# Planning the filler matmuls of a two-problem sliding-window attention by availability and deadline

## The chip, the cores and the metric

The kernel runs on one core of a Trainium2 chip. Its time is the device time in microseconds (us) of one launch; of several executions the median is given. A profile is one more execution, with the hardware profiler. Engines are named as in the profile: PE is TensorE's matmuls, PEld its weight loads, DVE is VectorE, ACT is ScalarE, POOL is GpSimd, and SP is SyncE, which here only issues DMAs.

## The reference

Two independent attention blocks, A and B, each with its own x (2048 x 1024), wqkv (1024 x 3072) and wo (1024 x 1024) in bf16; their outputs are put side by side into 2048 x 2048:

```
qkv = (x @ wqkv) -> q, k, v      # 32 heads of 32
scores = q k^T / sqrt(32)        # key j is seen by query i for 0 <= i - j < 256, else -1e9
out = softmax(scores) v -> (2048 x 1024) @ wo
```

With blocks of 128 positions, a query block sees its own key block (triangular mask), the one before (whole) and the one before that (the other triangle).

## The kernel before, in words

**Groups and sessions.** A group g is four heads of one problem (128 columns of q and of k), so there are 8 groups a problem and G = 16 in all. Of the 16 x 16 pairs of a key block j and a query block q, 45 are within the window (`entries`, L61). They are taken four at a time: a session. NS = 12 sessions make a group, the last of which has one pair alone, and the whole work is 192 sessions. `session` (L260) multiplies k by q for its four pairs and four heads into the PSUM tile st (one buffer, four banks; at most 32 small matmuls that run four at once in the array's row quarters), has ACT take the exp of all of it into pt (L280), and POOL zero the masked triangles (L285, L289). With one st the next session's scores wait for this exp.

**PV.** Two sessions (PV_LAG) after the last session that a chunk of 512 queries needs (k = 0 to 3, `ready`, L64), `pv` (L293) multiplies pt by V and by ones into the PSUM tile acc (one buffer, two banks), which gives the unnormalized output and the sums. DVE then normalizes in four pieces of 128 columns, a reciprocal (L321) and a multiply (L322) each. The first piece is issued at once; the others wait in the list `side` and are issued one at a time between fillers, after every 700 ns of them, or all together ahead of the next PV. There are 4 PVs in a group, in its sessions 4, 7, 10 and in session 1 of the next.

**Fillers.** All other matmuls (128 x 128 weights, 512 columns, planned at NS_MM = 216 ns) come in chains of 8 that accumulate into one of two PSUM tiles pp: QK chains (L133; 8 a group, one for q and one for k in each chunk of 512 positions, evicted by DVE with a cast, L146, and an OR into `top`, L148, from which `certify` reads at the end whether the values were small enough for an exp without a maximum), V chains (L153; 16 for each superblock m of four groups, evicted by ACT, L167) and output chains (L171; 32 a problem, evicted by ACT, L185, and stored by SP, L187).

**The planner.** TensorE runs in the order that the Python loop writes out. Each chain has a session from which it may start (`early`) and one by which it must be done (`late`); the list is sorted by `late`, and `start_chain` (L225) takes the first that may start. For each session the loop issues in this order: the chains that are due (`forced`), the scores, the PV that is due, the DMAs listed for it (`loads`), and then fillers until their planned time reaches a budget (`emit`, L234). The budget is max(NS_BASE = 1750 ns, `need`), where `need` (L251) is the largest rate that the deadlines ask for; it doesn't count what the session itself holds of scores and PV, nor whether the fillers will last. QK of group g may start with group g - 1, V of superblock m with the group before it, and A's output chains stand before V and QK chains of B by their deadlines. B's output chains have no deadline and begin once the last group's PVs are done; what is left of them when the 192 sessions are over is issued then.

**Loads.** x tiles (512 positions, transposed by the DMA, 1 MB, six buffers) and weights are issued on SP in the order of the listing, but each as soon as its buffer is free and what stands before it in SP's queue is issued. wqk is loaded for two groups at a time (512 KB for q and for k, pieces of 512 bytes); only the first such load is cut in two. At the start, the first half of wqk and V's first weights (1 MB) are issued on ACT's queue while SP issues the x tiles.

Of the kernel before, what the change touches and what calls it, by code (L numbers as in the profile page):

```python
# [18 lines left out]
P = 128  # L19
# [10 lines left out]
NS_BASE = 1750.0  # L30
PV_LAG = 2

# [19 lines left out]
def _fast_path(ctx, tc, cfg, problems, outs, consts, certify):  # L52
# [32 lines left out]
    zt = once.tile([P, 512], BF16, name="zt")  # L85
    nc.vector.memset(zt[:], 0.0)
    top = once.tile([P, 2, 512], BF16, name="top")
    nc.vector.memset(top[:], 0.0)
# [13 lines left out]
    def load_wqk(pair, queue, halves=(0, 1)):  # L102
        pi, t = divmod(2 * pair, T)
        if pair not in wqk:
            wqk[pair] = wqkp.tile([P, CT, 2, 256], BF16, name="wqk")
        if len(halves) == 2:
            cols = [(0, 256)]
        else:
            cols = [(128 * h, 128 * h + 128) for h in halves]
        for lo, hi in cols:  # L110
            for k in range(2):
                queue.dma_start(out=wqk[pair][:, :, k, lo:hi],
                                in_=wsrc(pi)[:, :, k, t * P + lo:t * P + hi])
# [19 lines left out]
    def qk_steps(g, which, k, lo=0, hi=512, st_=None, last=True):  # L133
        pi = g // T
        st_ = {} if st_ is None else st_
        steps = []
        for ct in range(CT):
            def f(ct=ct):
                if "pp" not in st_:
                    st_["pp"] = ps_proj.tile([P, 512], F32, name="pp")  # L140
                w_ = wqk[g // 2][:, ct, which, (g % 2) * P:(g % 2) * P + P]
                nc.tensor.matmul(st_["pp"][:, lo:hi], lhsT=w_, rhs=xT[(pi, k)][:, ct, lo:hi],  # L142
                                 start=(ct == 0), stop=(ct == CT - 1))
                if ct == CT - 1 and last:
                    dst = qk_tiles(g)[which][:, k * 512:(k + 1) * 512]
                    nc.vector.tensor_copy(out=dst, in_=st_["pp"][:])  # L146
                    seen = top[:, which, :].bitcast(I32)
                    nc.vector.tensor_tensor(out=seen, in0=seen, in1=dst.bitcast(I32),  # L148
                                            op=ALU.bitwise_or)
            steps.append((NS_MM * (hi - lo) / 512.0, f))  # L150
        return steps
# [53 lines left out]
    for m in range(NPROB * T // SB):  # L205
        for b in range(NB):
            k = b // QB
            g = m * SB
            early = NS * (g - 1) if k < 2 else pv_time(g - 1, k - 1) + 1
            chains.append(_Chain(early, pv_time(g, k), v_steps(m, b)))  # L210
    for pi in range(NPROB):
        for b in range(NB):
            k = b // QB
            osb = [None]
            early = pv_time(pi * T + T - 1, k) + 2
            late = 10 ** 6
# [4 lines left out]
    chains.sort(key=lambda c: c.late)  # L221

# [11 lines left out]
    def emit(now, budget):  # L234
        done = 0.0
        since = 0.0
        while done < budget and (current or start_chain(now)):
            ns, f = current.pop(0)
            f()
            done += ns  # L240
            since += ns
            if side and since >= 700.0:
                side.pop(0)()
                since = 0.0
        return done

    def forced(now):
        while any(c.late <= now for c in chains) or (current and current[0] is None):
            emit(now, NS_MM * CT if not current else NS_MM * len(current))

    def need(now):  # L251
        rate, work = 0.0, sum(ns for ns, _ in current)
        for c in chains:
            if c.late >= 10 ** 6:
                break
            work += NS_MM * CT
            rate = max(rate, work / (c.late - now)) if c.late > now else rate
        return rate
# [34 lines left out]
    def pv(g, k):  # L293
# [23 lines left out]
        rinv = misc.tile([P, 512], F32, name="rinv")  # L317
        for a in range(QB):
            def f(a=a):
                sl = slice(a * P, (a + 1) * P)  # L320
# [20 lines left out]
    for pair in range(2, G // 2):  # L341
        at(NS * (2 * pair - 2) + 1, lambda pair=pair: load_wqk(pair, nc.sync))
    for m in range(1, NPROB * T // SB):
        at(pv_time(SB * (m - 1), NQ - 1) + 1, lambda m=m: load_wv(m, nc.sync))
    for pi in range(1, NPROB):
        for k in range(NQ):
            now = NS * (pi * T - 3) + 2 * k if k < 2 else NS * (pi * T - 1) + first_use(k - 2, 0) + 1
            at(now, lambda pi=pi, k=k: load_x(pi, k))

    warm = ps_proj.tile([P, 512], F32, name="pp")  # L350
    for _ in range(11):
        nc.tensor.matmul(warm[:], lhsT=zt[:, 0:P], rhs=zt[:], start=True, stop=True)
# [6 lines left out]
    due = [(pv_time(g, k), g, k) for g in range(G) for k in range(NQ)]  # L359
    wo_next = 1  # L360
    certified = False
    for now in range(NS * G):
# [10 lines left out]
        emit(now, max(NS_BASE, need(now)))  # L373
        if not certified and g == G - 1 and not any(c.late < 10 ** 6 for c in chains):
            certify(top, ps_proj)
            certified = True
        if wo_next < NPROB and now >= NS * wo_next * T and not any(
                c.late < pv_time(wo_next * T + 1, 0) + 1 and c.early == pv_time(wo_next * T - 1, NQ - 1) + 2
                for c in chains) and not current:
            load_wo(wo_next)  # L380
            wo_next += 1
    end = NS * G
# [141 lines left out]
def kernel(  # L524
# [29 lines left out]
    def certify(top, pool):  # L554
        seen = top[:].rearrange("p a b -> p (a b)")
        nc.vector.tensor_single_scalar(out=seen.bitcast(I32), in_=seen.bitcast(I32),
                                       scalar=0x7FFF7FFF, op=ALU.bitwise_and)
# [51 lines left out]
```

## Time and profile before

| | |
|---|---|
| median of 3 runs | 739.2 us (737.25 to 740.1) |
| profiled execution | 739.39 us, of which the span from the first to the last instruction is 737.6 |
| PE busy | 646.8 us, 88% of the span |
| DVE, ACT, POOL busy | 449.9, 410.0, 301.5 us |
| mean granted clock of TensorE | 0.948 of full speed |
| time to the first exp, and from the last exp to the end | 19.7 us, 53.2 us |

The profile's page sums each engine's busy time, cuts the span into 40 slices and follows the chain of work that ended last. Queries to the same trace give the busy time in chosen windows, the instructions in order of time, and for each instruction how long its engine had been idle before it and what it waited for (in brackets). A busy PE isn't one at full rate: at half the granted clock the same matmuls are busy twice as long.

### The profile page before, as it was taken

The page shows a single profiled execution, that of the slowest core. Times are in us where ns is not written, and L with a number is a line of the kernel's source. Part 1 is how long each engine was busy: PE and PEld are TensorE (multiplying, and loading weights), DVE is VectorE, ACT ScalarE, POOL GpSimd, SP SyncE. Part 2 cuts the span into 40 slices and gives each one's busy share as a digit, 9 for nine tenths or more (in the row PEclk, how much of TensorE's full clock was granted, in tenths as well). Part 3 has the DMA queues.
Part 4 walks back from the last instruction along what each step waited for, and adds up shares of the span by engine and source line. Part 5 has one row for each costly group of instructions (what it writes and reads, how often), then busy time and mean ns, then how long its engine had stood idle before and what let it go on. Part 6 is the DMA issues. An engine that isn't in the chain of part 4 may idle for free.

```text
span 737.6 us, 15737 instructions
## 1 busy us (share of the span) xinstructions
PE 646.8 (88%) x6877; PEld 295.7 (40%) x6877; DVE 449.9 (61%) x776; ACT 410.0 (56%) x321; POOL 301.5 (41%) x484
## 2 busy tenths in 40 slices
PE   5999999589997867689999998997999998748996
PEld 2444344344443333334444443443444444324442
DVE  1363888665677759456325337997767799865500
ACT  0655555647564654645565665564768665657332
POOL 0333454634344543523233234454555555645100
PEclk8999999899999979699999999999999999868999
DMA  9900200600042005000300135002000000000111
GB/s 237 276 2 6 89 24 1 116 1 2 1 116 58 1 2 115 1 1 2 113 31 30 50 95 182 20 2 58 2 1 2 2 1 3 1 2 30 59 72 74
DMA packets 62715, 34.62 MB, mean 47 GB/s; under 512 B 38064, under 2 KB 56496, under 8 KB 62640
## 3 DMA queue, kind: packets, MB, share of 16 engines
q1 hardware_dynamic: 57424, 31.46, 15.3%
q10 hardware_dynamic: 5216, 2.10, 1.2%
q8 instruction: 55, 0.90, 0.5%
q14 instruction: 20, 0.16, 0.1%
HBM read 16.78 MB, written 8.39 MB: 34 GB/s over the span
## 4 chain that ended last, share of the span: by engine, by line
PE 66%; DVE 22%; ACT 8%; DMA 2%; issue 1%; SPq 0%; ACTq 0%
PE pp L142 17%; PE pp L181 15%; PE pp L164 14%; PE acc L311 13%; DVE rinv L321 11%; PE st L272 7%; ACT pt L280 7%; DVE oT L322 4%; DVE qT L146 3%; DVE kT L146 2%; DVE top L148 2%; DMA xT<-in_A_x_dram 2%; ACT vt L167 0%; ACT osb L185 0%; SPq L94 0%
## 5 line engine op out<-in xcount | busy, mean ns | idle before, releaser
L280 ACT ACTIVATE pt<-st 128x2048 bf16<-128x2048 f32 x192 | 340.0, 1771 | 234.5 <-PE st L272 226.4
L321 DVE RECIPROCAL rinv<-acc 128x128 f32<-128x128 f32 x256 | 243.1, 950 | 170.7 <-PE acc L311 170.7
L142 PE MATMUL pp<-xT,wqk 128*128 128x512 bf16 (+1 forms) x1040 | 251.1, 386 | 17.5 <-DMA xT<-in_A_x_dram 7.1
L289 POOL TENSOR_SCALAR_AFFINE_SELECT pt<-pt 128x512 bf16<-128x512 bf16 x224 | 147.8, 660 | 243.3 <-ACT pt L280 243.3
L285 POOL TENSOR_SCALAR_AFFINE_SELECT pt<-pt 128x512 bf16<-128x512 bf16 x256 | 167.5, 655 | 140.7 <-ACT pt L280 140.7
L142 PEld LDWEIGHTS <-wqk 128*128 128x128 bf16 x1040 | 96.2, 100 | 136.9 <-issue 44.6
L164 PE MATMUL pp<-wv,xT 128*128 128x512 bf16 x512 | 121.6, 380 | 3.6 <-DVE kT L146 1.7
L181 PE MATMUL pp<-wo_sb,oT 128*128 128x512 bf16 x512 | 116.9, 383 | 1.0 <-ACT osb L185 1.0
L272 PE MATMUL st<-qT,kT 32*128 32x256 bf16 (+2 forms) x1472 | 77.1, 281 | 44.7 <-ACT pt L280 40.4
L322 DVE TENSOR_TENSOR oT<-acc,rinv 128x128 bf16<-128x128 f32 x256 | 74.5, 291 | 8.8
L272 PEld LDWEIGHTS <-kT 32*128 32x128 bf16 x1472 | 26.6, 93 | 125.3 <-issue 118.2
L146 DVE CAST qT<-pp 128x512 bf16<-128x512 f32 x64 | 43.8, 684 | 53.3 <-PE pp L142 53.3
L181 PEld LDWEIGHTS <-oT 128*128 128x128 bf16 x512 | 48.7, 98 | 62.0 <-issue 7.6
L164 PEld LDWEIGHTS <-xT 128*128 128x128 bf16 x512 | 46.6, 98 | 63.5 <-issue 14.1
L311 PE MATMUL acc<-pt,vt 128*32 128x256 bf16 (+2 forms) x1664 | 57.2, 280 | 14.5 <-DVE oT L322 14.5
L185 ACT CAST osb<-pp 128x512 bf16<-128x512 f32 x64 | 37.2, 586 | 53.9 <-PE pp L181 50.3
L311 PE MATMUL acc<-pt,ones 128*32 128x256 bf16 (+2 forms) x1664 | 58.2, 283 | 0.0
L167 ACT CAST vt<-pp 128x512 bf16<-128x512 f32 x64 | 37.0, 585 | 25.9 <-PE pp L164 25.7
L311 PEld LDWEIGHTS <-vt 128*32 128x32 bf16 x1664 | 36.2, 102 | 35.0 <-issue 30.6
L146 DVE CAST kT<-pp 128x512 bf16<-128x512 f32 x64 | 43.7, 683 | 7.7 <-PE pp L142 7.7
L311 PEld LDWEIGHTS <-ones 128*32 128x32 bf16 x1664 | 40.1, 107 | 6.5 <-issue 1.3
L148 DVE TENSOR_TENSOR top<-top,kT 128x256 int32<-128x256 int32 x64 | 33.3, 520 | 2.2
(18 smaller groups left out, 43.6 us busy)
## 6 DMA issues: line engine op xcount, KB each, us to landing
out_dram<-osb SPq DMA_DIRECT2D x32, 256.0 KB, 2.0
wqk<-in_B_wqkv_dram SPq DMA_DIRECT2D x8, 512.0 KB, 4.7
wqk<-in_A_wqkv_dram SPq DMA_DIRECT2D x6, 512.0 KB, 5.3
wo_sb<-in_A_wo_dram SPq DMA_DIRECT2D x1, 2048.0 KB, 11.2
wv<-in_B_wqkv_dram SPq DMA_DIRECT2D x2, 1024.0 KB, 5.4
wo_sb<-in_B_wo_dram SPq DMA_DIRECT2D x1, 2048.0 KB, 10.0
wqk<-in_A_wqkv_dram ACTq DMA_DIRECT2D x4, 256.0 KB, 6.8
wv<-in_A_wqkv_dram ACTq DMA_DIRECT2D x2, 512.0 KB, 7.5
```

The lines of the kernel that those rows point to most:

```text
L142: nc.tensor.matmul(st_["pp"][:, lo:hi], lhsT=w_, rhs=xT[(pi, k)][:, ct, lo:hi], start=(ct == 0), stop=(ct == CT - 1))
L146: nc.vector.tensor_copy(out=dst, in_=st_["pp"][:])
L148: nc.vector.tensor_tensor(out=seen, in0=seen, in1=dst.bitcast(I32), op=ALU.bitwise_or)
L164: nc.tensor.matmul(st_["pp"][:], lhsT=xT[(pi, k)][:, ct, a * P:(a + 1) * P], rhs=wv[m][:, ct, :], start=(ct == 0), stop=(ct == CT - 1))
L181: nc.tensor.matmul(st_["pp"][:], lhsT=oTs[(pi, k)][:, ct, a * P:(a + 1) * P], rhs=wo_sb[pi][:, ct, ch * 512:(ch + 1) * 512], start=(ct == ...
L272: nc.tensor.matmul(st[:, r, a * P:b * P], lhsT=kT[32 * r:32 * r + 32, j * P:(j + 1) * P], rhs=qT[32 * r:32 * r + 32, q0 * P:(q0 + b - a) * P],
L280: nc.scalar.activation(out=pt[:, :, :n, :].rearrange("p r j q -> p r (j q)"), in_=st[:, :, :n * P], func=ACT.Exp, bias=-SHIFT, scale=cfg.s ...
L285: nc.gpsimd.affine_select(out=blk, in_=blk, pattern=[[0, 4], [1, P]], compare_op=ALU.is_ge, fill=0.0, base=0, channel_multiplier=-1)
L289: nc.gpsimd.affine_select(out=blk, in_=blk, pattern=[[0, 4], [-1, P]], compare_op=ALU.is_gt, fill=0.0, base=0, channel_multiplier=1)
L311: nc.tensor.matmul(acc[32 * r:32 * r + 32, which, o:o + n * P], lhsT=lhsT, rhs=pts[(g, s)][:, r, a:a + n, :], start=(x == 0), stop=(x == l ...
L321: nc.vector.reciprocal(out=rinv[:, sl], in_=acc[:, 1, sl])
L322: nc.vector.tensor_tensor(out=oTs[(pi, k)][:, t, sl], in0=acc[:, 0, sl], in1=rinv[:, sl], op=ALU.mult)
```

## The change

Five things are changed.

The budget: `level` gives each session max(need, cap). `need` is again the largest rate that deadlines ask for, now with the planned time of scores (NS_QK) and PVs (NS_PV for each small matmul column) counted in; `cap` is the smallest rate at which what may start up to any later session would be used up. From it the session's own scores and PV (`fixed`) are taken off, so that a session with a PV gets fewer fillers. A chain is begun only if at least half a matmul of budget is left.

The times of chains: V of a superblock may be computed from its weights' load on, which is up to a whole superblock ahead (8 V tiles instead of 6); QK chains are due a session earlier; A's output chains get later deadlines, up to the reload of wo, which stands at a fixed session (one more oT tile).

The normalization: one multiply for every two reciprocals, 256 columns instead of 128.

wqk is loaded for one group at a time (256 KB for q and for k, pieces of 256 bytes), listed two sessions before the group ahead of it ends.

The first loads: wqk of group 0 on ACT's queue, then all on SP in the order x 0 (two halves), V's weights, x 1, wqk of group 1, x 2, x 3, wo. `top` has half its columns and also serves as the operand of the warm-up matmuls.

```diff
-NS_BASE = 1750.0
+NS_QK = 430.0
+NS_PV = 56.0
...
-    opool = ctx.enter_context(tc.tile_pool(name="oT", bufs=NQ + 1))
+    opool = ctx.enter_context(tc.tile_pool(name="oT", bufs=NQ + 2))
-    vp = ctx.enter_context(tc.tile_pool(name="vt", bufs=NQ + 2))
+    vp = ctx.enter_context(tc.tile_pool(name="vt", bufs=2 * NQ))
...
-    def load_wqk(pair, queue, halves=(0, 1)):
...
+    def load_wqk(g, queue):
+        pi, t = divmod(g, T)
+        wqk[g] = wqkp.tile([P, CT, 2, P], BF16, name="wqk")
+        for k in range(2):
+            queue.dma_start(out=wqk[g][:, :, k, :], in_=wsrc(pi)[:, :, k, t * P:(t + 1) * P])
...
+    def wv_time(m):
+        return pv_time(SB * (m - 1), NQ - 1) + 1 if m else 0
+
+    def x_time(pi, k):
+        if pi == 0:
+            return -1
+        if k < 2:
+            return NS * (pi * T - 3) + 2 * k
+        return NS * (pi * T - 1) + first_use(k - 2, 0) + 1
...
-                late = NS * g + first_use(k, 1 - which)
-                early = NS * (g - 1)
-                if g == T and k >= 2:
-                    early = NS * (g - 1) + 6
+                late = NS * g + first_use(k, 1 - which) - (1 if g else 0)
+                early = max(NS * (g - 1), x_time(g // T, k) + 3)
...
-            early = NS * (g - 1) if k < 2 else pv_time(g - 1, k - 1) + 1
+            early = max(wv_time(m) + 2, x_time(m * SB // T, k) + 3) if m else 0
+            if m > 1:
+                early = max(early, pv_time(SB * (m - 1) - 1, min(k + 1, NQ - 1)) + 1)
+            chains.append(_Chain(early, pv_time(SB * m, k), v_steps(m, b)))
+    wo_time = [0] + [NS * (pi * T + T - 3) for pi in range(1, NPROB)]
...
-                late = pv_time((pi + 1) * T, k + 1) if k + 1 < NQ else pv_time((pi + 1) * T + 1, 0)
+                late = pv_time((pi + 1) * T, k + 2) if k + 2 < NQ else wo_time[pi + 1] - 1
...
+    fixed = [NS_QK] * END
+    for d, g, k in due:
+        if d < END:
+            fixed[d] += NS_PV * (2 * (3 * QB - (2 if k == 0 else 0)) + 2)
...
-        while done < budget and (current or start_chain(now)):
+        while done < budget - 0.5 * NS_MM and (current or start_chain(now)):
...
-            if side and since >= 700.0:
+            if side and since >= 3.5 * NS_MM:
...
+    def level(now):
+        held = sum(ns for ns, _ in current)
+        size = NS_MM * CT
+        need, cap = 0.0, float("inf")
+        base = 0.0
+        for d in range(now + 1, END + 1):
+            base += fixed[d - 1]
+            must = base + held + size * sum(c.late <= d for c in chains)
+            may = base + held + size * sum(c.early < d for c in chains)
+            need = max(need, must / (d - now))
+            cap = min(cap, may / (d - now))
+        return max(need, cap)
...
-                nc.vector.reciprocal(out=rinv[:, sl], in_=acc[:, 1, sl])
-                nc.vector.tensor_tensor(out=oTs[(pi, k)][:, t, sl], in0=acc[:, 0, sl],
-                                        in1=rinv[:, sl], op=ALU.mult)
+                nc.vector.reciprocal(out=rinv[:, h * P:(h + 1) * P],
+                                     in_=acc[:, 1, a * P:(a + 1) * P])
+                if h:
+                    sl = slice((a - 1) * P, (a + 1) * P)
+                    nc.vector.tensor_tensor(out=oTs[(pi, k)][:, t, sl], in0=acc[:, 0, sl],
+                                            in1=rinv[:], op=ALU.mult)
...
-    load_wqk(0, nc.scalar, halves=(0,))
+    load_wqk(0, nc.scalar)
     load_x(0, 0, parts=2)
-    load_wv(0, nc.scalar, parts=2)
+    load_wv(0, nc.sync, parts=2)
     load_x(0, 1)
-    load_wqk(0, nc.scalar, halves=(1,))
+    load_wqk(1, nc.sync)
     load_x(0, 2)
     load_x(0, 3)
-    load_wqk(1, nc.sync)
     load_wo(0)
...
+    for g in range(2, G):
+        at(NS * (g - 2) + first_use(NQ - 1, 0) + 1, lambda g=g: load_wqk(g, nc.sync))
...
-        emit(now, max(NS_BASE, need(now)))
+        emit(now, level(now) - fixed[now])
```

## Rows read from the trace of the kernel before

**Rows 1.** The page: PE's busy line, the granted clock by slice, the chain by engine.
```profile
PE 646.8 (88%) x6877; PEld 295.7 (40%) x6877; DVE 449.9 (61%) x776; ACT 410.0 (56%) x321; POOL 301.5 (41%) x484
...
PEclk8999999899999979699999999999999999868999
...
PE 66%; DVE 22%; ACT 8%; DMA 2%; issue 1%; SPq 0%; ACTq 0%
```

**Rows 2.** Windows (start, eight group pairs, tail): length; PE, PEld, DVE, ACT, POOL; clock; DMA; GB/s.
```profile
0.00:19.72 19.72, 10.54 (x52) 5.61 (x53) 3.08 (x8) 1.28 (x2) 0.21 (x4) 0.83 1.08 234
19.72:109.12 89.40, 86.31 (x849) 38.02 (x848) 54.89 (x95) 50.71 (x40) 38.18 (x60) 1.00 0.28 79
109.12:190.33 81.21, 70.37 (x810) 32.85 (x809) 59.15 (x102) 47.62 (x34) 37.96 (x61) 0.94 0.14 27
190.33:267.92 77.59, 63.94 (x777) 29.80 (x776) 53.02 (x91) 45.59 (x31) 37.47 (x60) 0.91 0.16 42
267.92:369.62 101.70, 86.46 (x869) 38.93 (x868) 58.14 (x102) 51.52 (x41) 37.26 (x60) 0.91 0.16 43
369.62:469.56 99.94, 96.72 (x948) 43.57 (x947) 49.49 (x85) 59.12 (x55) 37.16 (x60) 1.00 0.23 75
469.56:544.07 74.51, 66.45 (x797) 30.33 (x797) 60.19 (x105) 46.16 (x32) 38.06 (x60) 0.98 0.06 16
544.07:614.50 70.43, 68.07 (x813) 30.81 (x812) 55.20 (x96) 47.01 (x34) 37.94 (x60) 1.00 0.01 2
614.50:684.34 69.84, 50.79 (x704) 24.31 (x703) 49.48 (x87) 44.60 (x28) 36.58 (x59) 0.83 0.03 9
684.34:737.58 53.24, 47.13 (x267) 21.51 (x265) 7.28 (x13) 16.42 (x28) 0.64 (x1) 0.98 0.19 71
```

**Rows 3.** Chain pieces (start, us, what) and timeline rows: fillers, PVs, a session's turn.
```profile
482.60 1.13 PE acc L311 x40
...
689.79 1.43 PE acc L311 x56
691.22 40.27 PE pp L181 x186
...
460.55 0.40 PE L272 MATMUL st<-qT,kT 32*128 32x384 bf16 x8
...
461.08 1.88 ACT L280 ACTIVATE pt<-st 128x2048 bf16<-128x2048 f32 x1 [0.58 <-PE st L272]
```

**Rows 4.** Timeline after six sessions without fillers: a PV waits for its accumulator.
```profile
149.07 1.47 PE L311 MATMUL acc<-pt,vt 128*32 128x128 bf16 x28 [2.43 <-DVE oT L322]
...
155.23 1.88 ACT L280 ACTIVATE pt<-st 128x2048 bf16<-128x2048 f32 x1 [6.58 <-PE st L272]
```

**Rows 5.** Start (timeline), landings of x (L94), issues by line, one pair's load and landing.
```profile
14.91 3.57 PE L142 MATMUL pp<-xT,wqk 128*128 128x256 bf16 x16 [5.64 <-DMA xT<-in_A_x_dram]
19.27 0.40 PE L272 MATMUL st<-qT,kT 32*128 32x384 bf16 x8 [0.79 <-DVE kT L146]
...
DMA to landing us min/median/max: 6.0/7.9/12.6
...
wqk<-in_A_wqkv_dram ACTq DMA_DIRECT2D x4, 256.0 KB, 6.8
...
223.06 0.99 SPq L112 DMA_DIRECT2D wqk<-in_B_wqkv_dram  x2
...
DMA to landing us min/median/max: 3.9/4.5/5.2
```

**Rows 6.** Groups by line and shape, DVE: normalization, cast, OR.
```profile
L321 DVE RECIPROCAL rinv<-acc 128x128 f32<-128x128 f32 x256 | 243.1, 950 | 170.7 <-PE acc L311 170.7
L322 DVE TENSOR_TENSOR oT<-acc,rinv 128x128 bf16<-128x128 f32 x256 | 74.5, 291 | 8.8
L146 DVE CAST qT<-pp 128x512 bf16<-128x512 f32 x64 | 43.8, 684 | 53.3 <-PE pp L142 53.3
...
L148 DVE TENSOR_TENSOR top<-top,kT 128x256 int32<-128x256 int32 x64 | 33.3, 520 | 2.2
```

More of the change, by code (lines that the diff above doesn't have):

```diff
@@ L29 @@
 NS_MM = 216.0
-NS_BASE = 1750.0
+NS_QK = 430.0
+NS_PV = 56.0
 PV_LAG = 2
+FREE = 10 ** 6
 class _Cfg:
@@ L83, in _fast_path @@
     xT, wqk, wv, wo_sb, vts, oTs, qks, pts = {}, {}, {}, {}, {}, {}, {}, {}
[L85 to L88, printed above, removed]
+    top = once.tile([P, 256], I32, name="top")
+    nc.vector.memset(top[:], 0)
+    blank = top[:].bitcast(BF16)
     def load_x(pi, k, parts=1):
@@ L100, in wsrc @@
         return problems[pi][1].rearrange("(ct p) (k n) -> p ct k n", p=P, k=3)
-    def load_wqk(pair, queue, halves=(0, 1)):
[L103 to L113, printed above, removed]
+    def load_wqk(g, queue):
[3 more added lines that the diff above has]
+            queue.dma_start(out=wqk[g][:, :, k, :], in_=wsrc(pi)[:, :, k, t * P:(t + 1) * P])
     def load_wv(m, queue, parts=1):
@@ L140, in f @@
                     st_["pp"] = ps_proj.tile([P, 512], F32, name="pp")
-                w_ = wqk[g // 2][:, ct, which, (g % 2) * P:(g % 2) * P + P]
+                w_ = wqk[g][:, ct, which, :]
                 nc.tensor.matmul(st_["pp"][:, lo:hi], lhsT=w_, rhs=xT[(pi, k)][:, ct, lo:hi],
@@ L146, in f @@
                     nc.vector.tensor_copy(out=dst, in_=st_["pp"][:])
-                    seen = top[:, which, :].bitcast(I32)
-                    nc.vector.tensor_tensor(out=seen, in0=seen, in1=dst.bitcast(I32),
-                                            op=ALU.bitwise_or)
+                    nc.vector.tensor_tensor(out=top[:], in0=top[:],
+                                            in1=dst.bitcast(I32), op=ALU.bitwise_or)
             steps.append((NS_MM * (hi - lo) / 512.0, f))
@@ L215, in _fast_path @@
             early = pv_time(pi * T + T - 1, k) + 2
-            late = 10 ** 6
+            late = FREE
             if pi + 1 < NPROB:
-                late = pv_time((pi + 1) * T, k + 1) if k + 1 < NQ else pv_time((pi + 1) * T + 1, 0)
+                late = pv_time((pi + 1) * T, k + 2) if k + 2 < NQ else wo_time[pi + 1] - 1
             for ch in range(cfg.NCH):
@@ L221, in _fast_path @@
     chains.sort(key=lambda c: c.late)
+    due = [(pv_time(g, k), g, k) for g in range(G) for k in range(NQ)]
+    END = NS * G
+    fixed = [NS_QK] * END
+    for d, g, k in due:
+        if d < END:
+            fixed[d] += NS_PV * (2 * (3 * QB - (2 if k == 0 else 0)) + 2)
     current = []
@@ L241, in emit @@
             since += ns
-            if side and since >= 700.0:
+            if side and since >= 3.5 * NS_MM:
                 side.pop(0)()
                 since = 0.0
-        return done
     def forced(now):
[L248 to L258, printed above, removed]
+        while any(c.late <= now for c in chains):
+            emit(now, NS_MM * (len(current) or CT))
+        emit(now, NS_MM * len(current) if any(c.late <= now + 1 for c in chains) else 0.0)
+    def level(now):
[10 more added lines that the diff above has]
+        return max(need, cap)
     def session(g, s):
@@ L330, in at @@
         loads.setdefault(now, []).append(f)
-    load_wqk(0, nc.scalar, halves=(0,))
+    load_wqk(0, nc.scalar)
     load_x(0, 0, parts=2)
-    load_wv(0, nc.scalar, parts=2)
+    load_wv(0, nc.sync, parts=2)
     load_x(0, 1)
-    load_wqk(0, nc.scalar, halves=(1,))
+    load_wqk(1, nc.sync)
     load_x(0, 2)
     load_x(0, 3)
-    load_wqk(1, nc.sync)
     load_wo(0)
-    for pair in range(2, G // 2):
-        at(NS * (2 * pair - 2) + 1, lambda pair=pair: load_wqk(pair, nc.sync))
+    for g in range(2, G):
+        at(NS * (g - 2) + first_use(NQ - 1, 0) + 1, lambda g=g: load_wqk(g, nc.sync))
     for m in range(1, NPROB * T // SB):
-        at(pv_time(SB * (m - 1), NQ - 1) + 1, lambda m=m: load_wv(m, nc.sync))
+        at(wv_time(m), lambda m=m: load_wv(m, nc.sync))
     for pi in range(1, NPROB):
+        at(wo_time[pi], lambda pi=pi: load_wo(pi))
         for k in range(NQ):
-            now = NS * (pi * T - 3) + 2 * k if k < 2 else NS * (pi * T - 1) + first_use(k - 2, 0) + 1
-            at(now, lambda pi=pi, k=k: load_x(pi, k))
+            at(x_time(pi, k), lambda pi=pi, k=k: load_x(pi, k))
     warm = ps_proj.tile([P, 512], F32, name="pp")
     for _ in range(11):
-        nc.tensor.matmul(warm[:], lhsT=zt[:, 0:P], rhs=zt[:], start=True, stop=True)
+        nc.tensor.matmul(warm[:], lhsT=blank[:, 0:P], rhs=blank[:, 0:512], start=True, stop=True)
     held = [{}, {}]
@@ L357, in _fast_path @@
                 f()
-    due = [(pv_time(g, k), g, k) for g in range(G) for k in range(NQ)]
-    wo_next = 1
     certified = False
-    for now in range(NS * G):
+    for now in range(END):
         g, s = divmod(now, NS)
@@ L372, in _fast_path @@
             f()
-        emit(now, max(NS_BASE, need(now)))
-        if not certified and g == G - 1 and not any(c.late < 10 ** 6 for c in chains):
+        emit(now, level(now) - fixed[now])
+        if not certified and not current and not any(c.late < FREE for c in chains):
             certify(top, ps_proj)
             certified = True
[L377 to L382, printed above, removed]
+    assert certified
+    end = END
     emit(end, 2 * NS_MM * CT)
@@ L554, in certify @@
     def certify(top, pool):
-        seen = top[:].rearrange("p a b -> p (a b)")
-        nc.vector.tensor_single_scalar(out=seen.bitcast(I32), in_=seen.bitcast(I32),
-                                       scalar=0x7FFF7FFF, op=ALU.bitwise_and)
+        seen = top[:]
+        nc.vector.tensor_single_scalar(out=seen, in_=seen, scalar=0x7FFF7FFF, op=ALU.bitwise_and)
         nc.vector.tensor_reduce(out=pm[:], in_=seen.bitcast(I16), axis=AX.X, op=ALU.max)
```

9 lines of the change are left out of this document (5 added, 4 removed).

## The prediction

> **What bounds the kernel now.** I read the page's busy times first: TensorE is busy for 88% of the span, yet its clock row falls to 9, 7 and 6 in places, so part of that busy time is matmuls at half rate [rows 1]. The chain that ended last is 66% TensorE and 22% VectorE [rows 1]: TensorE is the bound, but not everywhere. The windows over pairs of groups show where: PE is busy 96 to 97% of groups 0-1, 8-9 and 12-13 and only 73% of groups 14-15, with granted clocks of 0.91 to 0.94 in groups 2 to 7 and 0.83 in 14-15 [rows 2]. So I price a session. A filler matmul takes 40.27/186 = 0.2165 us in the tail, the last one's longer end included (I take 0.2157 without it, 1.5 us less over 1880 fillers); a PV takes 1.43 us (1.13 for k = 0, which has 40 matmuls of 56), one session's scores take TensorE 0.40 us, and a session can't be shorter than one exp plus the turn to the next, 1.88 + 0.58 = 2.46 us [rows 3]. A session then lasts 0.40 + 0.2157 x fillers + PV, at least 2.46 us (1.18 for the twelfth, which has one tile). A pair of groups (24 sessions, 8 PVs) costs 20.1 us + 0.2157 x fillers, plus what its short sessions lack to the floor.
>
> Going through the planner's sums of before, session by session, gives 304, 208, 176, 268, 348, 196, 212 and 109 fillers in the eight pairs up to the last session's exp, and 33 dry sessions that get none: 6, 8, 7, 2 and 10 of them in pairs 2-3, 4-5, 6-7, 10-11 and 14-15. My rule gives 84.6, 73.5, 70.4, 88.9, 95.7, 66.1, 67.5 and 60.1 us, together 606.8: 552 of work and 55 by which sessions miss the floor. The windows measure 89.4, 81.2, 77.6, 101.7, 99.9, 74.5, 70.4 and 69.8 [rows 2]. The rest is 58 us: 4.8, 4.2 and 2.9 in the pairs without dry sessions (4.0 on average), 7 to 13 in the others. Why dry sessions cost more than the floor: the pieces that normalize a PV are put between fillers, so without fillers they are issued late; the next PV waited 2.43 us for its accumulator and the next exp 6.58 us [rows 4], at a granted clock of 0.94 over that pair [rows 2].
>
> **What the change does to the plan.** The budget of a session becomes max(need, cap) less its own fixed work. Example: at the first session of group 2, need is set by session 158: (120,676 ns fixed until then + 4 x 216 in hand + 163 chains due x 1728)/134 sessions = 3009 ns. Less 430 it makes 12 fillers, less 1886 in a session with a PV it makes 5. Done for all sessions (this is arithmetic of the diff): 308, 234, 204, 194, 277, 257, 205 and 202 fillers in the pairs, 9 dry sessions instead of 33 (the last 3 of group 4, 5 at the end of group 6, one in group 7, where V of the third superblock has to wait for B's later x tiles), and 151 fillers after the last exp instead of 211.
>
> **The sum.** First the sessions: 20.1 us (18.7 for the pair 0-1, with 7 PVs) + 0.2157 x fillers gives 85.1, 70.6, 64.1, 62.0, 79.9, 75.6, 64.3 and 63.3, 565 in all; 4.6, 8.5, 3.3 and 7.8 are added for the floor in pairs 4-5, 6-7, 12-13 and 14-15 (there 7 or 8 fillers, 2.15 us, lie under an exp turn of 2.46). That is 589.2 for 606.8.
>
> The rest of 58: 4.0 for each of eight pairs is 32; in the disturbed pairs 45.9 - 5 x 4.0 = 25.8 us fell on 33 dry sessions, 0.78 each, so 7 for nine. I take off 3 for the lighter VectorE (below): 36.
>
> The tail: 53.2 us from the last exp to the end [rows 2] less 60 x 0.2157 = 12.9: 40.3. The 60 chain steps aren't gone, they stand in the sessions above.
>
> The start: TensorE waited 5.64 us for the second half of x tile 0, which landed at 14.9 and put the first scores at 19.27 [rows 5]. Until then it shared the queues with V's weights and x tile 1, at 234 GB/s [rows 2]. Now x tile 0 (1.05 MB) and 0.52 MB of wqk come first: 1.57 MB from 2.3 us on is done at 9.0. Plus the 4.36 us from landing to scores, 13.4. V's weights, now behind x tile 0 on SP, need 4.5 us more, 13.5, as the first V chain wants them. So the start moves 5.9 us, to 13.8 for the first exp. Bounds: 3 if V's weights, with no second queue, land 3 us later; 7.5 if the clock doesn't drop in the wait, since the 16 half-width matmuls took 3.57 us after it, where 16 x 0.108 = 1.7 would do. A quiet x tile lands in 6.0 us [rows 5], so 9.0 beside half a tile of weights is the middle.
>
> 13.8 + 589.2 + 36.3 + 40.3 = 679.6 us of span. The profiled execution took 739.39 us for a span of 737.6, so 1.8 lies around it; its time is 0.2 over the median of 739.2. Forecast: 681 us.
>
> **Parts that I cost at little.** *One multiply for two reciprocals.* 256 multiplies of 128 columns at 291 ns become 128 of 256 columns. No row shows that form. It is between 291 and 582 ns; a cast of 512 columns takes 684 [rows 6], so a column costs (684 - 291)/384 = 1.02 ns and 256 columns 422. That takes 128 x 160 ns = 20 us off VectorE. It lies beside TensorE where that is the bound; where groups have nothing but QK chains VectorE is busy for 60.2 of 74.5 us [rows 2], and there it counts: I took 3 of 0 to 7. The accumulator is released in two steps instead of four; the last step is longer by 0.13 us, which counts only where the next PV waits.
>
> *The pieces' spacing.* 3.5 x 216 = 756 ns still means every fourth filler. With 12, 5 and 12 fillers around a PV all pieces are issued before the next PV, by the plan at all but 3 PVs; in before pieces were left at 9.
>
> *QK chains one session earlier, top at half its columns, the buffers.* The first takes away waits of scores for a cast, already inside the 36; a smaller check before the end is worth under 1 us, in the last group; two more V tiles and one more oT tile issue nothing.
>
> *wqk per group.* On SP 30 issues of 256 KB replace 14 of 512 KB; a pair of issues holds SP 0.99 us [rows 5]. Each waits for QK of group g-2, due by session 8, and is listed at session 10, so that it holds up nothing behind it (x loads, later the output stores). From there to the first use are two sessions, some 4.2 us at worst (6 fillers, one score tile, 12 fillers); a pair's 1 MB landed in 3.9 to 5.2 us [rows 5], half of that should land in less. Cost 0; up to 1 us per group if not.
>
> **Rivals.** *Late weights.* The pieces of wqk shrink from 512 to 256 bytes. On the ACT queue, with that width, 256 KB took 6.8 us against 3.9 to 5.2 for 512 KB on SP [rows 5], though in the crowd of the start. If width is why and it holds here too, each load of 14 groups comes 6.8 - 4.2 = 2.6 us late: 36 us, 717 us. Against: in before the SP queue ran ahead, so most loads should be issued long before the listed session. The Trainium skill, DMA: Bandwidth & Descriptors, Specifications, gives 512 B as the least transfer for line rate, below which the engine reads, modifies and writes: by it this rival holds wherever a load isn't early.
>
> *VectorE in step.* VectorE and TensorE are in order and hand casts and pieces to each other; at 12 fillers a session of QK chains, three sessions hold 4.6 + 3.6 x 1.2 = 9.0 us of VectorE in 9.2. If every pair then loses as much as the disturbed ones did (9.2 instead of 4.5), the rest is 74: 718 us. For it: groups 10-11, with 2 dry sessions, lost 8.4. Against: 4.2 in 8-9 with V and output chains mixed in, as most pairs now have.
>
> *Little left over.* Mixed groups at full flow lose as little as 2.9 a pair: rest 18, 662 us.
>
> *The plan doesn't hold.* If deadlines and data leave 20 dry sessions instead of 9, each costs (55 + 26)/33 = 2.4 us: 707 us.
>
> *Slower.* One accumulator serves all PVs. If, with PVs every third session and no slack between, VectorE finishes its pieces late everywhere, each of 64 PVs waits as the one in rows 4 did: at 2.43 us that is 155 us. It decides from 0.92 us a PV: 681 + 59 = 740. At 1 us it gives 745 us. Against it: 8 PVs in groups 8-9 with 9 to 18 fillers a session cost 4.2 us in all.
>
> **How the numbers follow.** The forecast 0.60 (its own range 666 to 695), little left over 0.13, VectorE in step 0.14, late weights 0.06, the plan 0.03, slower 0.04. 658 to 708 holds the forecast, little left over, the plan, and those outcomes of VectorE in step and late weights that stop halfway: some 0.8. Faster by over 0.5% (about what a measurement of this kernel can tell from no change) 0.95, within 0.5% 0.01, slower 0.04.
>
> **What would show it.** Exp intervals near 3.05 us through groups 2 to 6, in PV sessions as in others; no granted clock under full before the end of group 4 but for the start; first scores at 13 to 14 us; some 40 us after the last exp; VectorE some 20 us less busy; dry sessions in groups 4, 6 and 7 alone, with waits for the accumulator there. Wrong would be waits of QK matmuls for wqk at the start of groups, PVs that wait in dense groups, or long sessions with 12 fillers.

## The result and the profile after

The changed kernel takes 692.33 us (median of 4, 689.04 to 693.16) against 738.95: a ratio of 0.936, 95% interval 0.933 to 0.940. The profiled execution took 693.16 us, its span 691.4. Forecast were 681 us, within 658 to 708. Of the runs below, one execution of late_verdict (698.25 us) was in a slower state, with a granted clock of 0.937 where its other three had 0.981 to 0.985, and is left out of its median.

The page after: PE's busy line, the granted clock by slice, and the chain by engine.

```profile
PE 634.2 (92%) x6877; PEld 287.5 (42%) x6877; DVE 428.4 (62%) x647; ACT 408.7 (59%) x321; POOL 299.9 (43%) x484
...
PEclk9999999999987999789999999999999999998999
...
PE 67%; DVE 24%; ACT 5%; issue 1%; DMA 1%; POOL 1%; ACTq 0%
```

ACT's share of the chain fell from 8 to 5%, VectorE's rose from 22 to 24% [rows 1]. The clock row has three low places left: at groups 4-5, at groups 6-7 and, shorter, in group 15. The windows answer to [rows 2]: the start, eight pairs of groups, the tail (length; PE, PEld, DVE, ACT, POOL; clock; DMA; GB/s).

```profile
0.00:12.40 12.40, 8.59 (x52) 4.83 (x53) 2.50 (x7) 1.28 (x2) 0.20 (x4) 1.00 0.93 219
12.40:100.88 88.48, 86.70 (x853) 38.43 (x852) 53.72 (x83) 50.87 (x40) 37.82 (x60) 1.00 0.39 90
100.88:174.97 74.09, 72.23 (x835) 32.27 (x834) 55.28 (x84) 49.25 (x37) 37.26 (x60) 1.00 0.17 36
174.97:252.63 77.66, 70.96 (x805) 32.03 (x804) 52.56 (x80) 47.51 (x34) 37.67 (x60) 0.91 0.20 42
252.63:331.39 78.76, 68.07 (x795) 31.44 (x794) 52.91 (x80) 46.53 (x33) 37.44 (x60) 0.91 0.20 38
331.39:416.68 85.29, 81.64 (x878) 36.43 (x877) 53.35 (x79) 52.56 (x43) 37.84 (x60) 1.00 0.19 54
416.68:498.81 82.13, 77.70 (x858) 34.50 (x857) 55.40 (x82) 50.68 (x40) 37.81 (x60) 1.00 0.05 14
498.81:567.99 69.18, 66.03 (x806) 30.37 (x805) 45.32 (x66) 49.44 (x38) 37.21 (x60) 1.00 0.23 70
567.99:651.60 83.61, 68.27 (x798) 31.61 (x797) 52.81 (x83) 48.91 (x37) 36.07 (x59) 0.96 0.05 20
651.60:691.40 39.80, 34.03 (x207) 15.62 (x205) 4.56 (x7) 11.70 (x21) 0.63 (x1) 0.96 0.18 68
```

The start is 7.3 us shorter and the tail 13.4; the eight pairs took 664.6 us and now 639.2. Over the session rule of the prediction (85.1, 70.6, 68.7, 70.5, 79.9, 75.6, 67.6, 71.1 = 589.2) the pairs are by 3.4, 3.5, 9.0, 8.3, 5.4, 6.5, 1.6 and 12.5: 50 us, where 36 were forecast. Four sorts of place make them up.

First the two runs of dry sessions that the plan still has. Timeline at the start of group 5, after the dry end of group 4 (start, length, instruction, idle before it and what ended it):

```profile
209.43 4.75 PE L136 MATMUL pp<-xT,wqk 128*128 128x512 bf16 x12
...
216.40 1.04 PE L324 MATMUL acc<-pt,vt 128*32 128x128 bf16 x28 [1.89 <-DVE oT L341]
...
221.39 1.88 ACT L293 ACTIVATE pt<-st 128x2048 bf16<-128x2048 f32 x1 [4.87 <-PE st L285]
```

Twelve fillers take 4.75 us instead of 2.6, at the half clock that the dry sessions left behind; then the PV waits 1.89 us for its accumulator, as in [rows 4]. These two sessions, with 12 and 6 fillers, last 11.8 us where the rule says 6.1: of the 9.0 us of this pair, 5.7 lie in what follows its dry sessions.

Second the certificate, the check of the values near the end, in group 15:

```profile
620.51 0.19 PE L573 MATMUL pp<-okp,ones 128*1 128x1 f32 x2 [3.54 <-DVE okp L570]
...
621.18 7.96 PE L174 MATMUL pp<-wo_sb,oT 128*128 128x512 bf16 x24
```

A matmul that sums one number over the partitions stands in TensorE's order right behind VectorE's part and waits 3.54 us for it; the 24 fillers after it take 7.96 us, 0.33 each, mostly at half clock. The kernel before has the same matmul, but among its dry sessions:

```profile
650.22 0.19 PE L562 MATMUL pp<-okp,ones 128*1 128x1 f32 x2 [2.03 <-DVE okp L559]
```

There it waited 2.03 us, about as long as TensorE idles in a dry session anyway (2.06 us, for the exp).

Third VectorE in step with TensorE. Timeline in group 10, a full session without a PV:

```profile
436.45 1.75 DVE L337 RECIPROCAL rinv<-acc 128x128 f32<-128x128 f32 x2
...
438.24 0.42 DVE L341 TENSOR_TENSOR oT<-acc,rinv 128x256 bf16<-128x256 f32 x1
438.58 0.68 DVE L140 CAST qT<-pp 128x512 bf16<-128x512 f32 x1
...
439.31 1.67 PE L157 MATMUL pp<-wv,xT 128*128 128x512 bf16 x7 [0.92 <-DVE qT L140]
```

A q chain was done at about 436.5, but its cast stands in VectorE's order behind two reciprocals and a multiply and begins at 438.58. The next chain but one needs that pp tile, so TensorE waits 0.92 us. Thirteen full sessions of groups 1 to 11 are like it, 0.7 to 1.3 us longer than the rule, nine of them in groups 8 to 11. Over the whole trace, by the table of waits (us in total, times, longest):

```profile
PE acc L324 <- DVE oT L341: 10.7, 9, 2.0
...
PE pp L136 <- DVE qT L140: 4.6, 5, 1.1
...
PE pp L157 <- DVE qT L140: 3.1, 4, 0.9
PE pp L136 <- DVE kT L140: 3.0, 6, 0.9
...
PE pp L136 <- DMA xT<-in_A_x_dram: 1.5, 1, 1.5
```

Fourth the six PVs of groups 14-15 that stand before the certificate. Their sessions have one to three fillers and last 3.0 to 4.0 us over a floor of 2.46, 6.2 us too long in all; with 6.1 for the two sessions of the certificate that is the 12.5 of this pair. VectorE ahead of the first of them, which began at 571.76:

```profile
569.14 0.42 DVE L141 TENSOR_TENSOR top<-top,kT 128x256 int32<-128x256 int32 x1
569.49 1.76 DVE L337 RECIPROCAL rinv<-acc 128x128 f32<-128x128 f32 x2
571.28 0.42 DVE L341 TENSOR_TENSOR oT<-acc,rinv 128x256 bf16<-128x256 f32 x1
```

The last pieces stand behind a cast and an OR, and all six PVs begin 0.06 us after the multiply. (Two of the six, 2.9 us, are put down to a mask select of GpSimd, which ended 0.04 us after the multiply.)

### The profile page after: what moved, and what is told of

Same layout as the page of the kernel before. It is cut to its first block, busy times and chain, and to the rows that moved or that the text cites. A ratio compares the mean times of both kernels' runs of the same rounds, so it can differ in the third digit from the quotient of the medians.

```text
span 691.4 us, 15630 instructions
## 1 busy us (share of the span) xinstructions
PE 634.2 (92%) x6877; PEld 287.5 (42%) x6877; DVE 428.4 (62%) x647; ACT 408.7 (59%) x321; POOL 299.9 (43%) x484
## 4 chain that ended last, share of the span: by engine, by line
PE 67%; DVE 24%; ACT 5%; issue 1%; DMA 1%; POOL 1%; ACTq 0%
PE pp L174 16%; PE pp L136 16%; PE pp L157 15%; PE acc L324 13%; DVE rinv L337 11%; PE st L285 7%; ACT pt L293 5%; DVE top L141 4%; DVE qT L140 3%; DVE oT L341 3%; DVE kT L140 2%; DMA xT<-in_A_x_dram 1%; POOL pt L298 0%; ACT osb L178 0%; ACT vt L160 0%
## 5 line engine op out<-in xcount | busy, mean ns | idle before, releaser
L337 DVE RECIPROCAL rinv<-acc 128x128 f32<-128x128 f32 x256 | 231.1, 931 | 183.4 <-PE acc L324 183.2
L136 PEld LDWEIGHTS <-wqk 128*128 128x128 bf16 x1040 | 94.1, 99 | 132.6 <-issue 43.3
L174 PE MATMUL pp<-wo_sb,oT 128*128 128x512 bf16 x512 | 119.1, 386 | 0.5 <-ACT osb L178 0.5
L285 PE MATMUL st<-qT,kT 32*128 32x256 bf16 (+2 forms) x1472 | 74.9, 274 | 18.1 <-ACT pt L293 16.3
L324 PE MATMUL acc<-pt,vt 128*32 128x256 bf16 (+2 forms) x1664 | 53.1, 266 | 13.6 <-DVE oT L341 10.7
L341 DVE TENSOR_TENSOR oT<-acc,rinv 128x256 bf16<-128x256 f32 x128 | 54.3, 424 | 4.4
L324 PE MATMUL acc<-pt,ones 128*32 128x256 bf16 (+2 forms) x1664 | 53.9, 269 | 0.0
L324 PEld LDWEIGHTS <-ones 128*32 128x32 bf16 x1664 | 37.9, 101 | 4.6 <-issue 0.2
L141 DVE TENSOR_TENSOR top<-top,qT 128x256 int32<-128x256 int32 x64 | 36.2, 566 | 2.2
```

Source lines behind the costliest of these rows:

```text
L141: nc.vector.tensor_tensor(out=top[:], in0=top[:], in1=dst.bitcast(I32), op=ALU.bitwise_or)
L174: nc.tensor.matmul(st_["pp"][:], lhsT=oTs[(pi, k)][:, ct, a * P:(a + 1) * P], rhs=wo_sb[pi][:, ct, ch * 512:(ch + 1) * 512], start=(ct == ...
L285: nc.tensor.matmul(st[:, r, a * P:b * P], lhsT=kT[32 * r:32 * r + 32, j * P:(j + 1) * P], rhs=qT[32 * r:32 * r + 32, q0 * P:(q0 + b - a) * P],
L324: nc.tensor.matmul(acc[32 * r:32 * r + 32, which, o:o + n * P], lhsT=lhsT, rhs=pts[(g, s)][:, r, a:a + n, :], start=(x == 0), stop=(x == l ...
L337: nc.vector.reciprocal(out=rinv[:, h * P:(h + 1) * P], in_=acc[:, 1, a * P:(a + 1) * P])
```

## The experiments

Each kernel is an edit of the changed one (L numbers differ a little); the medians are of 4 runs (late_verdict's of 3). The kernel before, run beside each of three sets of them on the same chip, had medians of 738.5, 739.7 and 738.8.

**old_start**, the first loads as before:

```diff
-    load_wv(0, nc.sync, parts=2)
+    load_wv(0, nc.scalar, parts=2)
     load_x(0, 1)
-    load_wqk(1, nc.sync)
+    load_wqk(1, nc.scalar)
```

> The changed kernel with the first loads issued as before: V's first weights and the second wqk on ACT's queue beside the x tiles, instead of behind them on SP. My account: the first exp goes back from 12.4 to about 19 us and the rest is unchanged, so 692 + 7 = 699 us. Rival: what the start gives is lost again to later loads (x tiles 1 to 3 come later now), then 692 to 694 us.

Measured 699.71 us, first exp at 19.6, the pairs as in the changed kernel within 0.1 us but for 4-5 and 6-7 (2.5 and 1.6 shorter). By the medians the start is worth 7 us and is kept to the end; the profiled execution, the shortest of the four at 696.22, keeps only 3 us of it, as in groups 4 to 7 it had 17 us at half clock and the changed kernel 27.

**old_budget**, max(1750, need) and no look at supply:

```diff
+    def need(now):
...
-        emit(now, level(now) - fixed[now])
+        emit(now, max(1750.0, need(now)))
```

> The changed kernel with the old budget rule: max(1750 ns, the rate of the deadlines), the session's own PV not taken off and no look at supply. The new times of the chains stay. The plan then has 17 dry sessions instead of 9, PV sessions as full as others, and 216 chain steps after the last exp instead of 151. My account: the session rule gives 7 us more, 8 more dry sessions at 0.8 us another 6: 705 us. Rival: the new times of the chains (V a superblock ahead) are all that counts and the budget rule nothing: 692 to 695 us.

Measured 690.11 us: my account failed. The pairs were 91.1, 74.0, 75.2, 78.9, 83.4, 79.0, 73.3 and 65.7, the tail 53.9. The session rule, worked out for this plan, gives the 7 us more (12-13, with 20 fillers more: 3.5, measured 4.1), but the rest came out at 39 us instead of 50. The last pair and the tail together are 3.8 us shorter; the pair's eight dry sessions run near the floor, since none is followed by a crowd, and its PVs, with as many fillers beside them as any session, don't wait for the accumulator. In these runs a dry session has no price of its own; what follows it has.

**old_v**, V one group ahead:

```diff
-            early = max(wv_time(m) + 2, x_time(m * SB // T, k) + 3) if m else 0
-            if m > 1:
-                early = max(early, pv_time(SB * (m - 1) - 1, min(k + 1, NQ - 1)) + 1)
+            early = NS * (SB * m - 1) if k < 2 else pv_time(SB * m - 1, k - 1) + 1
```

> The changed kernel with V's chains allowed only one group ahead, as before; budget rule, V tiles and all else as changed. The plan has 15 dry sessions (groups 2, 5 and 6) instead of 9. My account: the rule gives 8 us more, 6 dry sessions another 5: 705 us. Rival: the budget rule alone levels the load and V's times are worth nothing: 692 to 695 us.

Measured 695.37 us, 3 more: nearer to the rival. The rule's 8 us are there (8.5 by the plan), and again the rest came out smaller, 46 us for 50.

**both_old**, the two edits above together:

> The changed kernel with both the old budget rule and V's old times: 23 dry sessions. Each alone gave 0 to 3 us. My account: the two stand in for each other, either one is enough to fill most dry sessions, and without both the rule and the late pieces cost about 10 us: 702 us. Rival: they add up, 692 + 3 - 2 = 693 us.

Measured 700.82 us. Each alone costs 3 us or nothing, both 8.5. By the session rule they would simply add, 7 and 8.5 to 15. Each alone, and both together, cost less than that; why both cost more than the sum of each was not tried.

**old_plan**, the whole plan of before (budget, all times of chains, rounding), with the new start, multiply and loads:

```diff
-                late = NS * g + first_use(k, 1 - which) - (1 if g else 0)
-                early = max(NS * (g - 1), x_time(g // T, k) + 3)
+                late = NS * g + first_use(k, 1 - which)
+                early = NS * (g - 1) + (6 if g == T and k >= 2 else 0)
...
-                late = pv_time((pi + 1) * T, k + 2) if k + 2 < NQ else wo_time[pi + 1] - 1
+                late = pv_time((pi + 1) * T, k + 1) if k + 1 < NQ else pv_time((pi + 1) * T + 1, 0)
```

> The changed kernel with the whole plan of before (budget rule, the times of QK, V and output chains, the rounding of a budget); what stays changed are the order of the first loads, the multiply for two reciprocals, wqk by groups and the reload of wo. If the parts add up, this is before less the start (7, from old_start) and less the multiply (12, from old_mult): 720 us, so that the plan as a whole is worth some 27 us and wqk by groups nothing. Rival: wqk by groups or the reload carry part of the gain: 710 us or less.

Measured 726.22 us: the plan as a whole is worth 34 us of the 47. Budget and V give 8.5 of them (both_old); the other 25 come with the times of QK and of A's output chains, the rounding of the budget and the finishing of a chain a session before it is due (the edit takes all four back), which were not parted. The sum with old_start and old_mult overshoots (7 + 12 + 34 = 53): under the old plan the start and the multiply, with the loads of wqk and wo, give 12.6 together, not 19.

**old_mult**, four multiplies:

```diff
-                if h:
-                    sl = slice((a - 1) * P, (a + 1) * P)
-                    nc.vector.tensor_tensor(out=oTs[(pi, k)][:, t, sl], in0=acc[:, 0, sl],
-                                            in1=rinv[:], op=ALU.mult)
+                sl = slice(a * P, (a + 1) * P)
+                nc.vector.tensor_tensor(out=oTs[(pi, k)][:, t, sl], in0=acc[:, 0, sl],
+                                        in1=rinv[:, h * P:(h + 1) * P], op=ALU.mult)
```

> The changed kernel with four multiplies of 128 columns for a PV instead of two of 256: VectorE 20 us more busy. My account: VectorE lies beside TensorE in most places, 3 us more (0 to 7): 695 us. Rival (VectorE and TensorE in step in the groups full of QK chains): each multiply delays a cast for which a chain waits, 10 us or more: 702 us.

Measured 704.31 us: 12 more, the rival's size, but not at its place. Groups 2 to 13 are 0.5 us a pair longer on average; groups 14-15 took 91.1 us instead of 83.6, at a granted clock of 0.89:

```profile
572.08:663.15 91.07, 71.89 (x788) 33.77 (x797) 56.69 (x99) 48.88 (x36) 36.07 (x59) 0.89 0.05 19
```

There the sessions have 7 or 8 fillers and one or two beside a PV, and the PV waits. The same PV, in session 1 of group 14, in the changed kernel and in old_mult:

```profile
571.76 0.84 PE L324 MATMUL acc<-pt,vt 128*32 128x128 bf16 x28 [1.44 <-DVE oT L341]
```

```profile
576.58 1.47 PE L324 MATMUL acc<-pt,vt 128*32 128x128 bf16 x28 [2.17 <-DVE oT L340]
577.81 1.52 PE L324 MATMUL acc<-pt,ones 128*32 128x128 bf16 x28
```

The wait is 0.7 us longer, and the PV after it is at half clock: 2.8 us for 1.43. Four of the six PV sessions there last 4.8 to 5.9 us instead of 3.5 to 4.0; the other two, where the clock held, are 0.24 us longer.

**taut**, cap instead of need where the supply bound comes first:

```diff
-            need = max(need, must / (d - now))
-            cap = min(cap, may / (d - now))
-        return max(need, cap)
+            if must / (d - now) > need:
+                need, need_at = must / (d - now), d
+            if may / (d - now) < cap:
+                cap, cap_at = may / (d - now), d
+        return cap if cap < need and cap_at < need_at else max(need, cap)
```

> The changed kernel with one rule of the budget turned round: where the supply bound (cap) is under the rate that the deadlines ask for (need) and its session comes first, the budget is cap and not need, so the fillers last. The plan has no dry session left (9 before), groups 1 to 6 get 10 or 11 fillers instead of 12 and none. My account: 13 us of missed floor and 9 x 0.8 us of late pieces go: 672 us. Rival, from the run with the old budget rule (17 dry sessions, and no slower): a dry session costs next to nothing, 688 to 692 us.

Measured 669.24 us, 23 less. Its windows of groups 4-5 and 6-7 (columns as above):

```profile
169.41:235.59 66.18, 63.38 (x793) 28.95 (x800) 53.04 (x81) 47.01 (x34) 37.33 (x60) 1.00 0.27 59
235.59:307.60 72.01, 68.85 (x817) 31.74 (x826) 53.18 (x82) 48.75 (x36) 36.50 (x60) 1.00 0.19 42
```

77.7 and 78.8 us became 66.2 and 72.0, at full clock throughout; the rest over the rule fell from 9.0 and 8.3 to 2.9 and 3.1. By the rule this plan needs 13 us less, as expected; the rest fell by another 10. So max(need, cap) hurries towards a deadline at session 158 while the supply ends at 88, and then has nothing.

**late_verdict**, the certificate's matmul in the tail:

```diff
-            certify(top, ps_proj)
+            certify(top)
...
     end = END
     emit(end, 2 * NS_MM * CT)
+    verdict(ps_proj)
...
```

> The changed kernel with the matmul of the certificate (which sums the check over the partitions) moved from the middle of group 15 to the tail; its VectorE part stays. In the trace this matmul waited 3.5 us for VectorE, and the 24 fillers after it ran at half the clock, 7.96 us instead of 5.2. My account: both go, 692 - 6 = 686 us. Rival: scores and exps wait for the same VectorE queue anyway and the clock falls all the same, 690 to 692 us.

Measured 685.04 us, 7 less. The same 24 fillers are now 5.35 us, and groups 14-15 took 77.5 us instead of 83.6, at full clock:

```profile
615.60 0.40 PE L285 MATMUL st<-qT,kT 32*128 32x384 bf16 x8 [0.42 <-ACT pt L293]
615.93 5.35 PE L174 MATMUL pp<-wo_sb,oT 128*128 128x512 bf16 x24
...
566.18:643.71 77.53, 63.81 (x787) 30.86 (x795) 52.66 (x82) 48.77 (x36) 36.07 (x59) 1.00 0.06 22
```

**no_or**, which leaves the OR out for all but the first two chains:

```diff
-                    nc.vector.tensor_tensor(out=top[:], in0=top[:],
-                                            in1=dst.bitcast(I32), op=ALU.bitwise_or)
+                    if g == 0 and k == 0:
+                        nc.vector.tensor_tensor(out=top[:], in0=top[:],
+                                                in1=dst.bitcast(I32), op=ALU.bitwise_or)
```

> The changed kernel without the OR into top for all but the first two QK chains (the check of the values then sees those alone): VectorE 68 us less busy. If VectorE in step with TensorE is what is left in the dense groups (the casts wait behind reciprocals, 13 us of waits for a cast and 11 for an accumulator in the trace), 10 to 15 us go: 680 us. Rival: the left-over comes from dry sessions, the certificate and the clock, and VectorE's length hardly counts: 689 to 692 us.

Measured 662.72 us, 30 less, over twice what I expected, for 70 us off VectorE. The waits for casts and accumulators add up to 21 us in the table above, but a late cast also delays scores and exps and lets the clock fall. Groups 10-11 lost 6.5 us over the rule, now 1.5, with TensorE 98% busy:

```profile
399.85:476.93 77.08, 75.58 (x850) 34.53 (x857) 44.33 (x65) 50.69 (x40) 36.35 (x60) 1.00 0.05 15
...
PE 82%; ACT 9%; DVE 4%; issue 2%; DMA 1%; POOL 0%; ACTq 0%
```

The second line is the chain that ended last: VectorE has 4% of it instead of 24. Of the thirteen long sessions one is left, and the six PV sessions of groups 14-15 are within 0.5 us of the floor.

**taut_verdict**, both edits:

> Both edits that helped together: budget = cap where supply comes first, and the certificate's matmul in the tail. They touch different groups (1 to 7 and 15), so 669 - 6 = 663 us. Rival: the 6 us of the certificate were a good pass of the clock, 667 us or more.

Measured 664.75 us (ratio 0.901, 0.898 to 0.903), 4.5 less than taut: between the sum and the rival. In the profiles groups 14-15 alone are 6 us shorter than in taut, so the two edits add up there.

**tv_spread**, taut_verdict with pieces after every fifth filler, counted across sessions:

```diff
-            since += ns
-            if side and since >= 3.5 * NS_MM:
+            since[0] += ns
+            if side and since[0] >= 4.5 * NS_MM:
...
```

> taut_verdict with the pieces of a PV put after every fifth filler instead of every fourth, counted on across sessions and not from each session's start. If casts wait because two reciprocals and a multiply stand ahead of them, spreading takes some of 14 us of such waits: 658 us. Rival: the last piece comes later, the next PV waits for the accumulator instead: 663 us or more.

Measured 664.13 us: no change. Against taut_verdict, TensorE's waits for a q cast rose from 7.5 to 9.6 us and those for a k cast fell from 5.0 to 2.9: this spread moves the waits from one cast to the other, and their sum stays at 12.5. No other spread was tried.

**tv_act_q**, taut_verdict with the q casts on ScalarE:

```diff
-                    nc.vector.tensor_copy(out=dst, in_=st_["pp"][:])
+                    if which == 0 and g:
+                        nc.scalar.copy(out=dst, in_=st_["pp"][:])
+                    else:
+                        nc.vector.tensor_copy(out=dst, in_=st_["pp"][:])
```

> taut_verdict with the casts of q chains (60 of 128 casts, all but group 0's) on ScalarE instead of VectorE: 41 us off VectorE, 35 us onto ScalarE. Without the ORs 68 us less of VectorE gave 30 us, so in step 41 us are worth 18: 645 us. Rival: a cast on ScalarE stands ahead of the next exp in its order and waits there for its chain, and every exp is late by a part of it: 660 us or more.

Measured 651.99 us (651.2 to 653.04), the fastest: 0.882 of before (0.880 to 0.884), and 40 us under the changed kernel. PE's busy line of its page:

```profile
PE 610.1 (94%) x6798; PEld 282.1 (43%) x6877; DVE 387.8 (60%) x587; ACT 438.6 (67%) x381; POOL 304.4 (47%) x484
```

VectorE is 43 us less busy than in taut_verdict. ScalarE is 30 us busier than in the changed kernel and its casts waited 9.6 + 4.8 us for TensorE, which costs less than the casts did on VectorE. The gain over taut_verdict is 13 us where the scale of no_or gave 18.

## Why the prediction was right, and what was 11 us off

The direction and the mechanism held: of the 46.2 us that the span lost, 7.3 are the start, 17.6 the sessions by the rule (606.8 to 589.2), 7.8 the rest (57.8 to 50.0) and 13.4 the tail. The plan came out as counted: 9 dry sessions, at the places named, and exp intervals of 3.03 to 3.05 us in sessions of 12 fillers. The terms, forecast and measured:

- Start: 13.8 and 12.4 us. The second half of x tile 0 was waited for 1.5 us instead of 5.64 [rows 5], and the clock no longer fell in that wait. The start moved 7.3 us for 5.9 forecast, near the upper of its bounds of 3 to 7.5 us, and for the reason given with that bound.
- Sessions by the rule: 589.2, taken as the yardstick for both.
- The rest: 36 and 50 us. This is the term that was mis-sized, by 14, and more than the whole of the miss.
- Tail: 40.3 and 39.8 us.

More than half of the 14 lies in groups 14-15: 12.5 us where an ordinary 4.0 was taken. "A smaller check before the end is worth under 1 us" was one wrong step: I priced its VectorE instructions and not the matmul that waits for them nor the clock behind it, 6 us by late_verdict's windows. In [rows 2] it hid among the dry sessions of groups 14-15. The other was the pieces: "all pieces are issued before the next PV, by the plan at all but 3 PVs" is so by the plan, but issued isn't done, and the six PV sessions there lost 6.2 us. "4.0 us for each of eight pairs" was the right size (3.4, 3.5, 5.4, 6.5 and 1.6 in the pairs without dry sessions or certificate), but it didn't fall by the 3 us taken off for the lighter VectorE, although old_mult puts some 4 us of the multiply on these five pairs; what took them back was not parted (the OR's longer runs, below, may be a part). "0.78 us for a dry session" was a mean over unlike things: in the two pairs with dry sessions the rest is 17.3 us, 9 over the 8 of two ordinary pairs. That is near the 7 forecast by luck, as old_budget shows dry sessions that cost nothing beyond the floor.

"3 of 0 to 7" for the lighter VectorE was wrong by old_mult: 12 us, of which 7.5 in groups 14-15. I let the multiply count only where TensorE's fillers are short of VectorE's work, and not where the next PV waits for the last piece, although I named that condition. The form itself was right: 422 ns worked out, 424 in the profile.

```profile
L341 DVE TENSOR_TENSOR oT<-acc,rinv 128x256 bf16<-128x256 f32 x128 | 54.3, 424 | 4.4
```

Of the rivals, *VectorE in step* is real: with VectorE 70 us lighter, 30 of the 50 us go (no_or). In the five ordinary pairs the rest falls from 20.4 to 7.5 us, so it sets most of the ordinary loss of 4 us a pair; that it did so in the kernel before as well is likely but was not tried. It didn't double that loss, which is why 718 us weren't reached. Two signs that were named as wrong came in part: PVs that wait in groups 14-15, and the thirteen full sessions that last too long.

*Late weights* didn't come: no matmul waited for wqk, whose loads of 256 KB landed in 3.1 to 6.0 us, each at least 6 us before its first use. The Trainium skill, DMA: Bandwidth & Descriptors, Specifications, gives 512 bytes as the least transfer for line rate. Here that decided nothing. It agrees in direction: by the pages 256 KB in pieces of 256 bytes landed in 3.6 and 3.8 us (medians for A and B), 512 KB in pieces of 512 bytes in 5.3 and 4.7, half as much time again per byte; a fixed part in each load would show the same and was not parted from it.

*The plan doesn't hold* was wrong, *little left over* too. *Slower* by PVs that wait each time didn't come: 9 PVs waited for the accumulator by the table, 10.7 us in all, and the two put down to GpSimd 2.9.

What stays open: which of the other parts of the plan (QK a session earlier, A's output chains later, the rounding, the chains finished a session early) carries the 25 us that old_plan shows beside budget and V; and why budget and V alone cost so much less than their rule.

## What to carry to other kernels

When work is levelled between a supply bound and a deadline bound, follow whichever comes first in time; hurrying for the far deadline when the near supply runs out cost the idle stretch, the clock after it and the work queued up behind it (23 us here). Price a small check by what waits for it in order, not by its own length. And an engine at 62% was worth 0.3 to 0.6 us for each one taken off it (tv_act_q, no_or, old_mult), when two in-order engines hand buffers to each other: take one part of its work away and look, before concluding from its share that it is off the path.

## What the runs showed of the hardware

The OR of two SBUF tiles (128 x 256 int32), the same instruction in both kernels, ran 424 to 902 ns in the trace before and 424 to 899 after, but its median rose from 426 to some 505 ns, so VectorE's gain from the multiply was partly taken back (mean 563 to 566 after, 506 to 520 before). The traces tell which engine it meets. An OR that no mask select of GpSimd overlapped in time took 424 to 427 ns every time, 53 of 128 before and 35 of 128 after; the others took 575 ns before and 617 after on average. The selects (128 x 512 bf16) are longer too, 696 ns with an OR beside them and 634 without, and in no_or, with two ORs left, 634 (683 at most). One OR by itself, then one with a select:

```profile
213.78 0.42 DVE L141 TENSOR_TENSOR top<-top,qT 128x256 int32<-128x256 int32 x1
...
439.29 0.68 DVE L141 TENSOR_TENSOR top<-top,qT 128x256 int32<-128x256 int32 x1
439.65 0.82 POOL L302 TENSOR_SCALAR_AFFINE_SELECT pt<-pt 128x512 bf16<-128x512 bf16 x1
```

So in the denser plan the two engines more often meet. Eleven of the 93 ORs that overlapped a select after the change still took 427 ns or less; what decides that was not tried.
